# A retention recurrence with a gated feed-forward: chunk 1's rows turned by DMA, q-state products as row tiles, some stores on ScalarE, another order and other PSUM banks

## The chip, the cores and the metric

The program runs on one core of one Trainium2 chip. Its engines are TensorE (PE in the profile; its weight loads are PEld), VectorE (DVE), ScalarE (ACT), GpSimd (POOL) and SyncE (SP), which here only issues DMA. The metric is the device time of one execution in microseconds (us), the median of several runs.

## The reference

Inputs q, k, v have the shape 4 batches x 8 heads x 768 positions x 64. Each head keeps a 64x64 state that decays by a constant per position; the outputs of the recurrence are normalised over the 512 channels of a position and go through a gated feed-forward with 1536 hidden channels.

```
for t in range(S):
    state = gamma * state + einsum('bhd,bhe->bhde', k[:, :, t], v[:, :, t])
    y[:, :, t] = scale * einsum('bhd,bhde->bhe', q[:, :, t], state)
x = y.transpose(0, 2, 1, 3).reshape(B * S, H * D)
xn = x / sqrt(mean(x * x, -1) + 1e-6) * rms_g
out = (silu(xn @ w_gate) * (xn @ w_val)) @ w_out
```

## The kernel before

The 768 positions are cut into 6 chunks of 128, and a piece of work is named by chunk and batch, `c.b`. Within a chunk the recurrence is attention with a decay mask; between chunks a state is carried. The text `ORDER` (lines 17 to 93) lists every operation in the order in which the code issues it; there is no scheduler behind it. Each engine works through its own operations in that order, and waits only where it reads what another engine writes, or overwrites what another engine still reads. A word such as `g.0.3.4.0.3/3` has the operation, its arguments, and behind the stroke the PSUM banks that its result gets; `@D`, `@A`, `@P`, `@S` name the engine VectorE, ScalarE, GpSimd or SyncE, where there is a choice. PSUM has eight banks, numbered 0 to 7 here, and a product that gets a bank waits until the last reader of that bank's former content is done. The operations that matter:

- `L` loads q, k or v (from POOL as bf16, from SP as float32); `Cq` and `V` then multiply q or v by its decay (`C`, lines 330 to 337; `V`, 345 to 356).
- `Tq`, `Tk` transpose on TensorE (lines 364 and 369), `Eq`, `Ek` copy the result out of PSUM; `tq`, `tk` do the same by a DMA transpose on SP's queue (line 385).
- `A` multiplies q and k (line 401, each head pair as two groups of 64 rows), `M0`, `M1` mask the result on VectorE (423).
- `Y` (lines 428 to 443) adds the product of mask and v (438) and the product of q and the carried state (442, four full-width matmuls per batch). `Z` (line 414) makes the latter for two batches at once in 16 matmuls on 64 rows each; a `Y` of such a pair has a fourth number and only the eight matmuls of line 433.
- `S` sums squares on ScalarE (455), `R` makes the root on POOL (465, 467), `N` writes the normalised rows xn on VectorE (479). `X` transposes xn on TensorE (492) and `XE@A`, `XE@D` copy it to xnT (500); `XE@S` does both by one DMA transpose (498), without `X`.
- `K` makes the state's increment (525), `U` adds it (534), `B` casts it (541).
- `g` and `v` are the two feed-forward products (549), with chunk, hidden blocks from and to, batches from and to; `s` is Silu on ScalarE (560), `h` the gated product hT on VectorE (568). Three buffers hold `s`.
- `d` and `e` are the output product (575, 597), `o` copies it out of PSUM (140), `st` stores it (588).
- `H` are matmuls without use in the result at the start.

Chunk c+1's recurrence runs between the feed-forward products of chunk c. A q or v load of chunk 2 on SP's queue waits for the last piece of w_out (line 313).

Of the kernel before, what the change touches and what calls it, by code (L numbers as in the profile page):

```python
# [27 lines left out]
wv.9.12 h.0.0.2.0.1 s.0.4.5.0.3 v.0.0.4.3.4/2 g.0.0.4.3.4/7 v.0.4.5.0.3/3 mc.1@P s.0.5.6.0.3 s.0.0.4.3.4 h.0.0.4.3.4
wo.0.4 v.0.5.6.0.3/4 h.0.5.6.0.3 D.1.1@P Lv.1.1@P h.0.4.5.0.3 Lv.1.0@P g.0.8.9.0.4/7 g.0.6.7.0.4/0 mc.0@D s.0.8.9.0.4
v.0.4.6.3.4/4 g.0.4.6.3.4/5 s.0.4.6.3.4 v.0.8.9.0.4/6 D.1.0@D D.1.2@P wo.4.8 s.0.6.7.0.4 Tk.1.2/2 Ek.1.2@D Tq.1.0/5  # L30
g.0.7.8.0.4/1 Eq.1.0@D h.0.8.9.0.4 v.0.6.7.0.4/7 h.0.4.6.3.4 wo.8.12 v.0.7.8.0.4/3 s.0.7.8.0.4 h.0.6.7.0.4
g.0.11.12.0.4/5 s.0.11.12.0.4 Tk.1.0/7 h.0.7.8.0.4 Tq.1.1/0 Lv.1.2@P Lq.1.3@P Tq.1.2/3 Eq.1.1@D B.0.1 Eq.1.2@D
g.0.9.10.0.4/4 s.0.9.10.0.4 B.0.2 g.0.10.11.0.4/2 s.0.10.11.0.4 Ek.1.0@D A.1.0/3710 M1.1.1 A.1.2/46 v.0.10.11.0.4/2
v.0.11.12.0.4/0 M0.1.2 M0.1.1 v.0.9.10.0.4/5 M0.1.0 Lv.2.0@S d.0.0.0.4/1 M1.1.0 M1.1.2 h.0.9.10.0.4 Y.1.1/3
d.0.3.0.4/6 Lk.2.3@P h.0.11.12.0.4 Y.1.0/4 S.1.1 Lk.1.3@P R.1.1 h.0.10.11.0.4 S.1.0 N.1.1 d.0.1.0.4/0 R.1.0
d.0.2.0.4/5 N.1.0 X.1.1/3 d.0.2.4.8 d.0.0.4.8 Lv.1.3@P d.0.3.4.8 X.1.0/7 d.0.3.8.12 XE.1.0@A Y.1.2/2 Tq.1.3/7
d.0.0.8.12 S.1.2 d.0.1.4.8 Lq.2.0@S XE.1.1@D o.0.0@A Eq.1.3@D o.0.3@A R.1.2 N.1.2 Tk.1.3/1 d.0.2.8.12 X.1.2/3 Ek.1.3@A
# [5 lines left out]
V.2.0@D tq.2.0 g.1.0.4.3.4/0 B.1.0 v.1.8.9.0.4/5 h.1.9.10.0.4 Cq.2.2@P Lq.3.0@S s.1.0.4.3.4 g.1.11.12.0.4/1 tk.2.1
s.1.8.9.0.4 h.1.0.4.3.4 g.1.5.6.0.4/7 Lv.2.1@S B.1.1 h.1.8.9.0.4 v.1.5.6.0.4/0 s.1.5.6.0.4 g.1.4.5.0.4/4
g.1.10.11.0.4/5 Cq.3.1@D Lv.2.2@S v.1.11.12.0.4/7 Cq.2.3@P h.1.5.6.0.4 s.1.11.12.0.4 B.1.3 h.1.11.12.0.4
v.1.10.11.0.4/0 s.1.10.11.0.4 s.1.4.5.0.4 h.1.10.11.0.4 v.1.4.5.0.4/4 Cq.3.0@P h.1.4.5.0.4 g.1.7.8.0.4/5 Lk.3.0@P
A.2.0/4726 tq.2.3 tq.2.2 M0.2.0 v.1.7.8.0.4/0 Lv.2.3@S tq.3.1 Lk.3.2@P M0.2.1 s.1.7.8.0.4 M1.2.1 g.1.6.7.0.4/1
# [25 lines left out]
tk.5.2 Y.4.3.2 Y.4.2.2 S.4.1 h.3.7.8.0.4 v.3.11.12.0.4/7 U.4.0.2@D V.5.1@A tk.5.3 Lv.5.3@S d.3.0.0.10/3 S.4.2 XE.4.0@S
h.3.11.12.0.4 S.4.3 Cq.5.0@P d.3.0.10.12 tq.5.1 R.4.3 N.4.3 o.3.0@A tq.5.0 d.3.2.0.12/1 R.4.1 d.3.1.0.10/2 o.3.2@A
tk.5.1 R.4.2 B.4.0 N.4.1 XE.4.3@S N.4.2 XE.4.2@S V.5.0@D B.4.1 A.5.2/3514 d.3.1.10.12 d.3.3.0.12/6 XE.4.1@S M1.5.2
g.4.8.9.0.4/0 tk.5.0 B.4.3 M1.5.3 M0.5.2 v.4.8.9.0.4/4 o.3.3@D V.5.3@P s.4.8.9.0.4 B.4.2 Y.5.2/5 M0.5.3 o.3.1@A
# [560 lines left out]
```

## Time and profile before

| what | value |
|---|---|
| median of 3 runs | 232.16 us (231.9 to 232.98) |
| the profiled execution | 231.99 us |
| its span, first to last instruction | 230.3 us |
| granted TensorE clock | 1.0 |
| busy TensorE, VectorE, GpSimd, ScalarE | 224.7, 127.8, 105.7, 84.2 us |

The profile has, for each instruction, its engine, its line and its times; the timeline gives start and duration, with the idle time of the engine ahead of it in brackets. The chain is followed back from the last instruction through what released each step. Durations of single matmuls overlap, so TensorE's work is read from the pieces of the chain and from starts. What ended an engine's idle time is inferred from semaphores.

### The profile page before, as it was taken

Reading aid. Unit: us, or ns where it says so; the run is one execution under the profiler, and the core shown is the slowest. Engines: PE = TensorE matmul, PEld = TensorE weight load, DVE = VectorE, ACT = ScalarE, POOL = GpSimd, SP = SyncE. Lnnn points to the kernel's source line nnn. Section 1 sums busy time; section 2 is a strip of 40 time slices with the busy share of each in tenths; the row PEclk is TensorE's granted clock in tenths of the full one; section 3 lists DMA queues with packets and bytes.
Section 4 is the critical chain, followed back from the end, with each engine's and each line's share of the span. In section 5 each row is a group of like instructions: output and inputs, shape, how many; then the busy total and the mean of one; then the engine's idle time right before and its main releaser. Section 6 shows DMA issues by size and latency. Waiting matters only on the chain.

```text
span 230.3 us, 4745 instructions
## 1 busy us (share of the span) xinstructions
PE 224.7 (98%) x1849; PEld 118.9 (52%) x1849; DVE 127.8 (55%) x232; ACT 84.2 (37%) x190; POOL 105.7 (46%) x177
## 2 busy tenths in 40 slices
PE   8889999999999999999999999999999999999994
...
GB/s 130 162 175 134 187 176 191 199 192 134 141 180 164 156 110 180 215 187 228 184 84 288 177 179 271 132 85 90 49 23 198 101 0 0 0 16 35 45 181 92
DMA packets 105352, 31.51 MB, mean 137 GB/s; under 512 B 94449, under 2 KB 102385, under 8 KB 105330
## 3 DMA queue, kind: packets, MB, share of 16 engines
...
q8 instruction: 14, 0.23, 0.4%
q14 instruction: 8, 0.07, 0.1%
...
## 4 chain that ended last, share of the span: by engine, by line
PE 93%; DVE 2%; DMA 2%; POOL 1%; issue 0%; ACT 0%; POOLq 0%; DVEq 0%
PE v_ps L549 27%; PE g_ps L549 27%; PE o_ps L575 26%; PE a_ps L401 2%; PE y_ps L438 2%; DMA qb<-in_q_dram 2%; PE y_ps L442 2%; PE kv_ps L525 1%; PE o_ps L597 1%; DVE am L423 1%; PE t_ps L369 1%; PE xt_ps L492 1%; DVE kd L514 1%; PE t_ps L364 1%; POOL qb L307 1%; PE g_row_ps L290 0%
## 5 line engine op out<-in xcount | busy, mean ns | idle before, releaser
L568 DVE TENSOR_TENSOR hT<-sg,v_ps 128x512 bf16<-128x512 bf16 (+2 forms) x76 | 48.0, 656 | 55.4 <-PE v_ps L549 40.2
L560 ACT ACTIVATE sg<-g_ps 128x512 bf16<-128x512 f32 (+2 forms) x76 | 42.3, 575 | 93.6 <-PE g_ps L549 85.2
L549 PE MATMUL g_ps<-xnT,wg_b 128*128 128x512 bf16 (+2 forms) x344 | 71.1, 344 | 0.0
L549 PE MATMUL v_ps<-xnT,wv_b 128*128 128x512 bf16 (+2 forms) x344 | 71.0, 344 | 0.0
L575 PE MATMUL o_ps<-wo_b,hT 128*128 128x512 bf16 x276 | 63.4, 379 | 0.0
L549 PEld LDWEIGHTS <-wg_b 128*128 128x128 bf16 x344 | 30.6, 98 | 29.9 <-issue 0.3
L549 PEld LDWEIGHTS <-wv_b 128*128 128x128 bf16 x344 | 30.5, 98 | 29.1 <-DVE hT L568 0.2
L575 PEld LDWEIGHTS <-hT 128*128 128x128 bf16 x276 | 26.3, 98 | 29.7
L465 POOL TENSOR_SCALAR ms<-ssq 128x1 f32<-128x1 f32 x24 | 4.5, 188 | 42.0 <-ACT xsq L455 41.1
L423 DVE TENSOR_TENSOR am<-a_ps,causal 128x512 bf16<-128x512 f32 x32 | 20.1, 684 | 3.2 <-PE a_ps L401 3.2
L479 DVE SCALAR_TENSOR_TENSOR xn<-y_ps,rstd,g_bc 128x512 bf16<-128x512 f32 x22 | 16.4, 749 | 9.8 <-POOL rstd L467 8.0
L541 POOL CAST st_b<-st_f 64x256 bf16<-64x256 f32 x40 | 18.1, 452 | 5.4 <-DVE st_f L534 4.1
L455 ACT ACTIVATE xsq<-y_ps 128x512 f32<-128x512 f32 x22 | 13.1, 598 | 15.6 <-PE y_ps L442 14.1
L309 POOL DMA_DIRECT2D kb<-in_k_dram x20 | 18.4, 921 | 0.0
L140 ACT COPY o_sb<-o_ps 128x512 f32<-128x512 f32 (+1 forms) x15 | 8.4, 568 | 24.0 <-PE o_ps L575 23.7
L337 POOL TENSOR_TENSOR qb<-qf,ydec 128x512 bf16<-128x512 f32 x13 | 13.9, 1069 | 5.0 <-DMA qf<-in_q_dram 2.3
L467 POOL TENSOR_TENSOR rstd<-ms,mhalf 128x1 f32<-128x1 f32 x24 | 13.3, 555 | 2.0
L140 DVE COPY o_sb<-o_ps 128x512 f32<-128x512 f32 (+2 forms) x11 | 6.7, 622 | 13.3 <-PE o_ps L575 7.6
L356 POOL TENSOR_TENSOR vp<-vf,vdec 128x512 bf16<-128x512 f32 x9 | 9.3, 1046 | 3.7 <-DMA vf<-in_v_dram 3.5
L423 DVE TENSOR_TENSOR am<-a_ps,mask 128x512 bf16<-128x512 f32 x16 | 9.9, 682 | 1.6 <-PE a_ps L401 1.5
L438 PEld LDWEIGHTS <-am 128*128 128x128 bf16 x176 | 7.7, 98 | 3.5
L234 PE MATMUL hot_ps<-one 128*128 128x512 bf16 x23 | 7.9, 491 | 1.1 <-DVE one L147 1.1
...
## 6 DMA issues: line engine op xcount, KB each, us to landing
...
```

The source lines that it names most:

```text
L140: return (e.copy if e is ACT else e.tensor_copy)(out, in_)
L309: i = done[n, c, b] = e.dma_start(out=x, in_=rows[n][b, c])
L337: e.tensor_tensor(out=u["qb"], in0=u["qf"], in1=ydec[:, c, :, None].to_broadcast([128, H, D]), op=ALU.mult)
L423: return DVE.tensor_tensor(out=u["am"][:, i], in0=u["a"][i], in1=m, op=ALU.mult)
L455: return ACT.activation(xsq, flat(u["y"]), AF.Square, accum_out=u["ssq"])
L467: return POOL.tensor_tensor(out=u["rstd"], in0=ms, in1=mhalf, op=ALU.pow)
L479: return DVE.scalar_tensor_tensor(out=u["xn"], in0=flat(u["y"]), scalar=u["rstd"], in1=g_bc, op0=ALU.mult, op1=ALU.mult)
L541: POOL.tensor_copy(st_b[b][r, :, i * 64:i * 64 + 64], st_f[b // 2][r, b % 2])
L549: r = nc.tensor.matmul(p[:, (n - n0) * m:(n - n0 + 1) * m], W[w][0][:, s, n * 128:(n + 1) * 128], xnT[c][:, s, b0 * C:b1 * C], start=s == ...
L560: return ACT.activation(sg[:, :cols], done["wg", c, n0, b0][:, :cols], AF.Silu)
L568: return DVE.tensor_tensor(out=hT[c][:, n0:n1, b0 * C:b1 * C], in0=sg, in1=p, op=ALU.mult)
L575: nc.tensor.matmul(o_ps[c, b], hT[c][:, n, b * C:(b + 1) * C], wo_b[:, n, :], start=n == 0, stop=n == NFF - 1)
```

## The change

The code is the same; the text `ORDER` is another. It has the same operations but for these:

- `X.1.0` to `X.1.3` are gone, and `XE.1.0` to `XE.1.3`, two on ScalarE and two on VectorE before, are now `@S`, DMA transposes.
- `Z.2.0`, `Z.3.0`, `Z.4.0` and `Z.5.2` are new, and their eight Y take the shorter form; with `Z.4.2`, which was there, five pairs have their q-state products as row tiles.
- Fourteen `st` move from `@S` to `@A`; four `Cq` go from POOL to VectorE and some `V` and `o` change engines.
- `Tk.1.3`, the transpose of chunk 1's last k, stands in both orders, on TensorE.
- Up to `M0.1.0` the sequence is the same and only the banks differ; behind it the sequence is another.

The diff is one of the table alone. Some of its lines: its first, the one with `g.0.3.4.0.3` in the head, one of chunk 1's feed-forward, and two with a new Z:

```diff
-Lk.0.2@S H.4/4 yd causal Lv.0.2@S>causal yt rms.1@S ident Ck.0.2@A Lq.0.0@P H.8/1 Lq.0.1@P Lq.0.2@P Tk.0.2/7 H.2/5
...
-v.0.3.4.0.3/3 v.0.2.3.0.3/4 N.0.3 g.0.3.4.0.3/0 Lk.1.2@P s.0.0.2.0.1 X.0.3/6 v.0.0.2.0.1/5 XE.0.3@A Lk.1.0@P B.0.0
...
-U.1.2.2@D d.0.1.8.12 Cq.2.1@P s.1.3.4.0.3 U.1.0@D g.1.2.3.0.3/2 v.1.0.1.0.3/5 N.1.3 Lq.3.1@S s.1.1.2.0.3 X.1.3/3
...
+Lk.0.2@S H.4/0 yd causal Lv.0.2@S>causal yt rms.1@S ident Ck.0.2@A Lq.0.0@P H.8/1 Lq.0.1@P Lq.0.2@P Tk.0.2/0 H.2/1 Lk.0.0@P
...
+v.0.2.3.0.3/6 N.0.3 g.0.3.4.0.3/3 Lk.1.2@P s.0.0.2.0.1 X.0.3/5 v.0.0.2.0.1/2 XE.0.3@A Lk.1.0@P B.0.0 wg.9.12
...
+v.1.2.3.0.3/2 v.1.1.2.0.3/0 Cq.2.1@D s.1.3.4.0.3 s.1.0.1.0.3 Lk.2.1@P XE.1.3@S Lq.2.3@S Lk.2.0@P tq.2.1 h.1.3.4.0.3
+Cq.2.3@D g.1.10.11.0.4/5 s.1.1.2.0.3 s.1.2.3.0.3 g.1.8.9.0.4/6 v.1.0.4.3.4/7 tq.2.0 h.1.1.2.0.3 h.1.0.1.0.3 Lk.3.0@P
...
+h.1.5.6.0.4 A.2.2/2317 Lv.2.3@S Lv.2.2@S Lk.3.1@P Z.2.0/64 Lq.3.0@S M1.2.0 Y.2.1.2 V.2.2@D h.1.7.8.0.4 M0.2.2 tk.3.1
...
+s.2.5.6.0.4 Z.3.0/21 s.2.2.3.0.4 Y.3.0.2 v.2.4.5.0.4/0 h.2.7.8.0.4 Lv.3.3@S V.3.1@D h.2.5.6.0.4 s.2.1.2.0.4
```

In the head, TensorE's rows from the last v product ahead of `g.0.3.4.0.3` on (this one is the product of line 549 with wg; the brackets name the semaphores that a row waits for, DMASW of a load, DVE of VectorE):

```order
 L549 MATMUL v_ps<-xnT,wv_b 128x384
 L549 LDWEIGHTS wg_b [waits DMASW6_49]
+L549 MATMUL g_ps<-xnT,wg_b 128x384 [waits DVE_49]
+L549 LDWEIGHTS wg_b
 L549 MATMUL g_ps<-xnT,wg_b 128x384
```

With bank 3 in place of bank 0, the product waits for VectorE.

SP's queue behind the three transfers of the start, before (vf and qf are loads of chunks 2 and 3, kT and qT their transposes):

```order
L309 DMA vf<-in_v_dram 128x8x64
L309 DMA qf<-in_q_dram 128x8x64 x3
L385 DMA_TRANSPOSE kT<-kb 128x4x128
L309 DMA qf<-in_q_dram 128x8x64
L385 DMA_TRANSPOSE kT<-kb 128x4x128
```

And after, at the same place:

```order
L498 DMA_TRANSPOSE xnT<-xn 128x4x128
L309 DMA vf<-in_v_dram 128x8x64
L309 DMA qf<-in_q_dram 128x8x64
L498 DMA_TRANSPOSE xnT<-xn 128x4x128 x2
L309 DMA qf<-in_q_dram 128x8x64 x2
L498 DMA_TRANSPOSE xnT<-xn 128x4x128
L309 DMA qf<-in_q_dram 128x8x64
L385 DMA_TRANSPOSE qT<-qb 128x4x128 x3
```

The four transposes of chunk 1's rows are new there, and the loads of q stand between and behind them; the last of the four q loads is `Lq.2.3`.

VectorE at the start of chunk 1's feed-forward, before, from the two masks of batch 3 (`M1.1.3`, `M0.1.3`) on:

```order
L423 TENSOR_TENSOR am<-a_ps,mask_102 128x512 x2
L534 TENSOR_TENSOR st_f_121<-st_f_121,kv_ps 128x256
L534 TENSOR_TENSOR st_f_122<-st_f_122,kv_ps 128x512
L534 TENSOR_TENSOR st_f_121<-st_f_121,kv_ps 128x256
L479 SCALAR_TENSOR_TENSOR xn<-y_ps,rstd,g_bc 128x512
L568 TENSOR_TENSOR hT<-sg,v_ps 128x384
L140 COPY xnT<-xt_ps 128x4x128
L568 TENSOR_TENSOR hT<-sg,v_ps 128x384 x3
```

And after:

```order
L423 TENSOR_TENSOR am<-a_ps,mask_102 128x512 x2
L140 COPY o_sb<-o_ps 128x512
L534 TENSOR_TENSOR st_f_122<-st_f_122,kv_ps 128x512
L140 COPY o_sb<-o_ps 128x512
L534 TENSOR_TENSOR st_f_121<-st_f_121,kv_ps 128x256
L479 SCALAR_TENSOR_TENSOR xn<-y_ps,rstd,g_bc 128x512
L337 TENSOR_TENSOR qb<-qf,ydec 128x512
L568 TENSOR_TENSOR hT<-sg,v_ps 128x384
L337 TENSOR_TENSOR qb<-qf,ydec 128x512
L568 TENSOR_TENSOR hT<-sg,v_ps 128x384 x3
```

Two `o`, and the q products `Cq.2.1` and `Cq.2.3`, now stand on VectorE among the first h of chunk 1; the copy of xnT is gone.

More of the change, by code (lines that the diff above doesn't have):

```diff
@@ L28 @@
[L28 to L37, printed above, removed]
@@ L43 @@
[L43 to L47, printed above, removed]
@@ L73 @@
[L73 to L76, printed above, removed]
-A.5.0/2067 Y.5.3/3 S.5.3 h.4.8.9.0.4 g.4.0.1.0.4/4 M0.5.1 M1.5.1 v.4.7.8.0.4/1 M1.5.0 M0.5.0 g.4.7.8.0.4/7 S.5.2
@@ new lines @@
+v.0.5.6.0.3/4 h.0.5.6.0.3 D.1.1@P Lv.1.1@P h.0.4.5.0.3 Lv.1.0@P g.0.8.9.0.4/6 g.0.6.7.0.4/4 mc.0@D s.0.8.9.0.4
+v.0.4.6.3.4/3 g.0.4.6.3.4/6 s.0.4.6.3.4 v.0.8.9.0.4/0 D.1.0@D D.1.2@P wo.4.8 s.0.6.7.0.4 Tk.1.2/6 Ek.1.2@D Tq.1.0/2
+g.0.7.8.0.4/4 Eq.1.0@D h.0.8.9.0.4 v.0.6.7.0.4/6 h.0.4.6.3.4 wo.8.12 v.0.7.8.0.4/0 s.0.7.8.0.4 h.0.6.7.0.4
+g.0.11.12.0.4/4 s.0.11.12.0.4 Tk.1.0/6 h.0.7.8.0.4 Tq.1.1/0 Lv.1.2@P Lq.1.3@P Tq.1.2/3 Eq.1.1@D B.0.1 Eq.1.2@D
+g.0.9.10.0.4/2 s.0.9.10.0.4 B.0.2 g.0.10.11.0.4/0 s.0.10.11.0.4 Ek.1.0@D A.1.0/2634 M1.1.1 A.1.2/51 v.0.10.11.0.4/7
@@ new lines @@
+v.3.9.10.0.4/2 h.3.1.2.0.4 s.3.6.7.0.4 v.3.4.5.0.4/5 g.3.3.4.0.4/0 h.3.0.1.0.4 Lq.4.3@S Lk.4.2@P h.3.6.7.0.4 B.3.3
+s.3.9.10.0.4 tk.4.1 tq.4.0 v.3.3.4.0.4/6 o.2.3@A g.3.4.5.0.4/4 B.3.1 Cq.4.3@P st.2.2@A tq.4.1 st.1.0@A s.3.3.4.0.4
+s.3.4.5.0.4 Lv.4.0@S h.3.3.4.0.4 h.3.9.10.0.4 B.3.2 Lq.4.2@S g.3.2.3.0.4/0 h.3.4.5.0.4 tk.4.0 A.4.0/4261 Lv.4.2@S
+Z.4.0/37 g.3.10.11.0.4/5 M1.4.1 s.3.2.3.0.4 V.4.0@P Lv.4.1@S M1.4.0 v.3.2.3.0.4/1 M0.4.1 Lq.5.3@S g.3.8.9.0.4/2
+Cq.4.2@P M0.4.0 s.3.8.9.0.4 v.3.10.11.0.4/4 s.3.10.11.0.4 tk.4.2 tq.4.3 tq.4.2 V.4.2@P Y.4.0.2 Lv.4.3@S h.3.2.3.0.4
@@ new lines @@
+v.3.8.9.0.4/2 S.4.0 tk.4.3 g.3.7.8.0.4/5 s.3.7.8.0.4 g.3.11.12.0.4/1 R.4.0 h.3.8.9.0.4 Lq.5.2@S Cq.5.3@P h.3.10.11.0.4
+s.3.11.12.0.4 V.4.3@A Lv.5.3@S V.5.3@P N.4.0 A.4.2/5426 V.4.1@D d.2.0.0.10/0 Y.4.1.2 M0.4.2 K.4.0.2/5 K.4.2.2/1 M1.4.2
+Cq.5.2@P S.4.1 M1.4.3 M0.4.3 Z.4.2/26 Y.4.3.2 U.4.2.2@D U.4.0.2@D B.4.0 v.3.7.8.0.4/4 Y.4.2.2 h.3.7.8.0.4 tk.5.2
+d.2.0.10.12 v.3.11.12.0.4/5 st.1.3@A S.4.3 R.4.3 tk.5.3 h.3.11.12.0.4 d.3.0.0.10/4 tq.5.2 N.4.3 R.4.1 N.4.1
+d.3.3.0.12/5 XE.4.0@S o.2.0@A S.4.2 tq.5.3 XE.4.3@S A.5.2/7301 R.4.2 XE.4.1@S N.4.2 XE.4.2@S d.3.1.0.10/6 tk.5.1
```

106 lines of the change are left out of this document (54 added, 52 removed).

## The prediction

> **What bounds the kernel now.** I read the page's busy shares first, then the chain that ended last, then, place by place, the timeline of TensorE beside that of the engine that hands over to it.
>
> ```profile
> PE 224.7 (98%) x1849; PEld 118.9 (52%) x1849; DVE 127.8 (55%) x232; ACT 84.2 (37%) x190; POOL 105.7 (46%) x177
> ...
> PE   8889999999999999999999999999999999999994
> ...
> PE 93%; DVE 2%; DMA 2%; POOL 1%; issue 0%; ACT 0%; POOLq 0%; DVEq 0%
> ```
>
> TensorE is busy in every slice behind the head, and 93% of the chain is TensorE itself. What a busy TensorE delivers is seen in the pieces of the chain (start, duration, line, number of matmuls):
>
> ```profile
> 60.42 0.22 PE xt_ps L492 x4
> ...
> 74.95 0.61 PE a_ps L401 x16
> 75.56 0.97 PE v_ps L549 x4
> 76.53 0.86 PE g_ps L549 x4
> ...
> 82.33 0.23 PE y_ps L438 x8
> 82.57 0.22 PE y_ps L442 x4
> ...
> 148.11 0.63 PE kv_ps L525 x32
> 148.74 0.34 PE y_ps L414 x16
> 149.08 0.97 PE v_ps L549 x4
> ...
> 182.15 2.59 PE g_ps L549 x12
> ```
>
> Twelve 512-column matmuls in 2.59 us are 0.216 us each, and a group of four takes 0.86 everywhere from 17 us to the end: before has no stall there to win back. The time is the sum of TensorE's work plus what a new order makes it wait. So there are two questions: how much work goes, and where TensorE now waits.
>
> **Work that goes.** The four X of chunk 1 (16 transposes) go: 4 x 0.22 = 0.88 us. Eight Y lose their four L442 matmuls (8 x 0.22 = 1.76), and four new Z add 0.34 each (1.36): 0.40 less, of which Z.3.0, standing alone between full-width products, gives back 0.11 (the product behind a 64-row group takes 0.97, not 0.86; Z.2.0, Z.4.0 and Z.5.2 lie against an A that pays this already): 0.28. K.1.1, now alone between two d pieces, costs a change in and out, an estimate of twice 0.11; K.2.2.2 joins the other K of chunk 2 and saves 0.1: +0.15 with the small rest. Together -1.0 us, with an error of 0.2.
>
> The row prices two tiles of q-state products at 0.34 against 0.44 for the full-width pair. The Trainium skill (TensorEngine Tiling (Array Packing), Theoretical Speedup) allows up to 2x for a contraction of 64; by it a Z would take 0.22 and the sum would come out 0.5 lower. The same page (Key Properties) says that a change of tiling mode drains the array, which speaks against scattered Z; the 0.11 behind L414 agrees with it. The sum goes by the rows.
>
> **Waits in the head.** Up to `M0.1.0` the operations are the same, but their PSUM banks are not: the head of after uses seven banks (bank 7 first at `v.0.10.11.0.4/7`), so a product often gets a bank whose reader has not finished. For each reuse I took the end of the reader and the start of the product from the timelines of before:
>
> ```profile
> 19.28 0.41 DVE L568 TENSOR_TENSOR hT<-sg,v_ps 128x256 bf16<-128x256 bf16 x1
> 19.93 0.42 DVE L140 COPY xnT<-xt_ps 128x512 bf16<-128x512 bf16 x1 [0.24 <-PE xt_ps L492]
> 21.92 0.75 DVE L479 SCALAR_TENSOR_TENSOR xn<-y_ps,rstd,g_bc 128x512 bf16<-128x512 f32 x1 [0.74 <-POOL rstd L467]
> 28.21 1.69 DVE L568 TENSOR_TENSOR hT<-sg,v_ps 128x512 bf16<-128x512 bf16 x3 [1.66 <-ACT sg L560]
> 33.39 0.41 DVE L140 COPY kT<-t_ps 128x512 bf16<-128x512 bf16 x1
> 34.32 0.67 DVE L568 TENSOR_TENSOR hT<-sg,v_ps 128x512 bf16<-128x512 bf16 x1
> ...
> 19.51 0.39 PE L492 MATMUL xt_ps<-ident,xn 128*128 128x128 bf16 x4
> 20.41 0.28 PE L549 MATMUL g_ps<-xnT,wg_b 128*128 128x128 bf16 x2
> 22.17 0.81 PE L549 MATMUL g_ps<-xnT,wg_b 128*128 128x384 bf16 x4
> 33.47 1.89 PE L549 MATMUL v_ps<-xnT,wv_b 128*128 128x512 bf16 x8
> 36.22 0.73 PE t_ps L369 x12
> ```
>
> A product starts 0.05 us behind the end it waits for (copy done 20.35, product 20.41). Then:
> - `X.0.0/5` gets the bank of `v.0.0.2.2.3/5`, read until 19.69: it starts at 19.74, not 19.50: +0.24.
> - `g.0.3.4.0.3/3` gets the bank of Y.0.3, whose reader N.0.3 ends at 22.67 (POOL sets that, so it doesn't move): 22.72, not 22.17 + 0.24: +0.31. TensorE is now 0.55 late.
> - VectorE's queue from 28.2 on starts with a wait on ScalarE's reading of a g product, so it moves by the same 0.55. `v.0.6.7.0.4/6` waits for the kT copy, 33.80 + 0.55 + 0.05 = 34.40, not 33.47 + 0.55: +0.38.
> - `v.0.7.8.0.4/0` (the second four of the eight at 33.47) waits for the hT product that ends at 34.99 + 0.55 + 0.05 = 35.59, not 34.33 + 0.93: +0.33.
> - The transposes at 36.22 hold 0.07 of an old wait (three times 0.22 is 0.66), which vanishes.
>
> Sum +1.2 us; nothing ahead of the product stream swallows it. Its bounds: 0 if the readers were all earlier for a reason I don't see, 1.6 if VectorE's queue slips more.
>
> **Waits at chunk 1's rows.** In before the rows reach xnT by TensorE and a copy; now by `XE.1.*@S`. From Y.1.3 to the end of its N, before:
>
> ```profile
> 56.33 0.40 PE L438 MATMUL y_ps<-vp,am 128*128 128x64 bf16 x8
> ...
> 57.07 0.60 ACT L455 ACTIVATE xsq<-y_ps 128x512 f32<-128x512 f32 x1 [0.70 <-PE y_ps L442]
> ...
> 58.19 0.56 POOL L467 TENSOR_TENSOR rstd<-ms,mhalf 128x1 f32<-128x1 f32 x1
> ...
> 58.79 0.75 DVE L479 SCALAR_TENSOR_TENSOR xn<-y_ps,rstd,g_bc 128x512 bf16<-128x512 f32 x1 [1.74 <-ACT sg L560]
> 61.40 1.49 DVE L568 TENSOR_TENSOR hT<-sg,v_ps 128x384 bf16<-128x384 bf16 x3
> ```
>
> That is 59.54 - 56.33 = 3.21 us. DMA times, first of all xnT transposes, then of those at 111 to 120, then of all q loads, then of the two q loads at 58 to 64, and the q product on VectorE (ns):
>
> ```profile
> L498 SPq DMA_TRANSPOSE xnT<-xn x16: 1189/1207/1801, 83.2 to 175.5; - x16
> DMA to landing us min/median/max: 2.4/2.5/5.2
> ...
> DMA to landing us min/median/max: 3.8/4.7/5.2
> ...
> L337 DVE TENSOR_TENSOR qb<-qf,ydec x3: 678/684/781, 68.2 to 140.9; 128x512 bf16<-128x512 f32 x3
> DMA to landing us min/median/max: 3.3/4.5/6.5
> ...
> DMA to landing us min/median/max: 3.3/3.3/3.4
> ```
>
> - Batch 2: from Y.1.2 to `g.1.2.3.0.3` the new order has 6.5 us of TensorE work (five d pieces of 0.86, two Y of 0.45, two transposes of 0.22, A at half of 0.61, K at three quarters of 0.63). Needed: 3.2 + 2.4 to 5.2. Slack 0.9 to -1.9; at the median 0.8.
> - Batch 3: from Y.1.3 to `g.1.10.11.0.4` 0.45 + 0.86 + 8 x 0.65 = 6.5. The same slack.
> - VectorE: `Cq.2.3@D` now stands ahead of three h, and its load `Lq.2.3@S` behind `XE.1.3@S` in SP's queue. From Y.1.3: 3.21 + 1.2 (the issue of XE) + load + 0.68 + two h of 0.5, then TensorE's `g.1.0.4.3.4/4` takes the bank that the second h frees; with hops of 0.1 that is 6.2 + load against 6.5 + 0.86 + 0.86 + 0.89 + 0.86 = 10.0. A load of 3.8 is free; 3.3 leaves 0.5, the median 4.5 costs 0.7, the longest 6.5 costs 2.7.
>
> I take +0.3 for the three together, because the rows nearest in time (3.3) are harmless; bounds 0 and +2.7.
>
> **Other handovers.** Behind chunk 3's last Y, TensorE has 36 x 0.216 + 0.45 = 8.2 us before `g.3.1.2.0.4`; needed are 3.2 + 1.2 (XE.3.3 ahead of XE.3.2 in the queue) + 2.4 to 5.2: slack 1.4 to -1.4. Chunks 2 and 5 are alike. I take +0.2, bounds 0 and +2.
>
> **Edits at nothing.** Fourteen stores are issued by ScalarE:
>
> ```profile
> L588 SPq DMA_DIRECT2D out_dram<-o_sb x26: 332/447/1516, 89.6 to 227.5; - x26
> ```
>
> Their issue on ScalarE isn't in the trace; on SP it takes 0.33 to 1.52 us. ScalarE is 37% busy, and its idle time between Silus hides it; a Silu queued behind a store delays h and a bank. Bounds: 0, and 14 x 0.45 = 6 us if every one lay on the path; I take 0, the row of the last copies being near: st.5.3.2 is issued before o.5.3.0 can start. The last transfer is again 192 columns, so the tail keeps its shape. Tk.1.3 stays on TensorE in both orders, so "its last k" costs and gives nothing. V and Cq change places between POOL and VectorE, neither of them the bound.
>
> **Sum.** The profiled execution took 231.99 us (span 230.3). 231.99 - 1.0 + 1.2 + 0.3 + 0.2 = 232.7; the median of before lies 0.17 above that execution, so 232.8.
>
> **Rivals.**
> - Slower by VectorE's wait for `Lq.2.3`: one mechanism, at `Cq.2.3@D`. It decides when the load takes over 4.8 us (then 1 us more than my sum, 233.8); at 6.5 it gives 235.3. For it: the median load of 4.5. Against: 3.3 at just this time. 0.14.
> - Slower by handovers of chunks 2, 3 and 5 with landings as at 111 to 120: some 2 us, 234.6. For it: 3.8 to 5.2 there. Against: 2.4 where DMA is idle. 0.18.
> - Faster, since the bank waits of the head are covered by something: 231.99 - 1.0 + 0.2 = 231.2, a little lower with a better tail. Against: the wait stands in the program, and the reader's end is set by other engines. 0.12.
> - Z at half price: 232.3, which changes no sign; L414's own row is against it. 0.02.
>
> **How the numbers follow.** My forecast has 0.54. A half per cent, 1.16 us, is about what a measurement of this kernel can tell from no change: faster is below 231.0, slower above 233.3. Faster: most of the third rival, 0.10. Slower: the first two, 0.32. The rest, 0.58, within. The range runs from 231.2 (no head waits) to 234.8 (the handovers, or a load of 6). The forecast's own is 231.9 to 233.3.
>
> **What would show it.** Right: TensorE idle for about 0.3 us each behind xn at 22.7, behind the kT copy near 34.3 and hT near 35.5; L492 with 16 fewer matmuls; Z groups at 0.34; a 512-column matmul still at 0.216. Wrong: no TensorE wait before 40 us (then faster); VectorE idle on a q load near 62 to 65 us with TensorE idle behind it, or long waits at the first products of chunks 3 and 5 (then slower); ScalarE's queue held by stores.

## The result, and the profile after

| kernel | median | executions | ratio to before, 95% interval |
|---|---|---|---|
| before | 232.09 us | 231.9 to 232.98 | |
| changed | 235.79 us | 234.69 to 236.39 | 1.0143, 1.011 to 1.0176 |

The change makes the kernel 1.4% slower; the time lies above the range of the prediction. Medians here and below are of all executions of a kernel, ratios leave out those more than 1.5% above its fastest. The profiled execution of the changed kernel took 234.69 us (span 233.0), the shortest of its four. Its page, by busy shares, slices and the chain that ended last:

```profile
PE 223.4 (96%) x1865; PEld 116.5 (50%) x1865; DVE 129.5 (56%) x242; ACT 83.8 (36%) x198; POOL 102.5 (44%) x180
...
PE   7799999999999999899998999999999999999994
...
PE 78%; DMA 9%; DVE 5%; POOL 3%; ACT 2%; issue 1%; SPq 1%; POOLq 0%; ACTq 0%
```

TensorE's busy time is less (223.4 against 224.7 us), but its share of the chain fell from 93% to 78%, and DMA's rose from 2% to 9%. TensorE now waits, and two of its 40 slices in the middle are no longer full. The timeline of TensorE shows where (in brackets the idle time ahead of a row and what is taken to have ended it; a wait inside a row only makes the row longer):

```profile
22.39 0.81 PE L549 MATMUL g_ps<-xnT,wg_b 128*128 128x384 bf16 x4
...
33.54 2.20 PE L549 MATMUL v_ps<-xnT,wv_b 128*128 128x512 bf16 x8
...
56.98 1.30 PE L549 MATMUL g_ps<-xnT,wg_b 128*128 128x384 bf16 x7 [0.51 <-DMA xnT<-xn]
...
94.17 1.02 PE L549 MATMUL v_ps<-xnT,wv_b 128*128 128x512 bf16 x4 [1.54 <-ACT o_sb L140]
...
127.09 1.67 PE L549 MATMUL g_ps<-xnT,wg_b 128*128 128x512 bf16 x7 [1.05 <-DMA xnT<-xn]
```

The last three are the first feed-forward products of chunks 1, 2 and 3: `g.1.2.3.0.3`, `v.2.3.4.0.4` and `g.3.1.2.0.4`. Counted from start to start, less the usual length of the group ahead, they wait 0.67, 1.72 and 1.21 us. In the head, row by row against before, the only new wait over 0.14 us is inside the eight matmuls at 33.54 (2.20 where 1.89 is usual): 0.31. Sum 3.9 us. `e.5.3.0`, the last output product, starts 2.53 us later than before (228.48 against 225.95), so 1.4 us of work went: chunk 1's X 1.0, Y 1.7 less 1.2 for the new Z, and 0.2 at A less 0.3 at v.

The chain of the changed kernel has the rows of chunks 1 and 3, with the transposes in it:

```profile
51.98 0.75 DVE xn L479
...
52.76 4.09 DMA xnT<-xn
...
56.98 0.32 PE g_ps L549
...
123.06 3.89 DMA xnT<-xn
...
127.09 1.02 PE g_ps L549 x4
```

And VectorE's timeline has the ends of N, from which each transpose can start (750 ns for a full row, L479), and in the head the readers of the banks:

```profile
21.59 0.75 DVE L479 SCALAR_TENSOR_TENSOR xn<-y_ps,rstd,g_bc 128x512 bf16<-128x512 f32 x1 [0.36 <-POOL rstd L467]
...
33.05 0.41 DVE L140 COPY kT<-t_ps 128x512 bf16<-128x512 bf16 x1
...
33.98 1.60 DVE L568 TENSOR_TENSOR hT<-sg,v_ps 128x512 bf16<-128x512 bf16 x3
...
88.32 0.75 DVE L479 SCALAR_TENSOR_TENSOR xn<-y_ps,rstd,g_bc 128x512 bf16<-128x512 f32 x1 [0.95 <-POOL rstd L467]
...
117.95 0.75 DVE L479 SCALAR_TENSOR_TENSOR xn<-y_ps,rstd,g_bc 128x512 bf16<-128x512 f32 x1
...
120.66 0.75 DVE L479 SCALAR_TENSOR_TENSOR xn<-y_ps,rstd,g_bc 128x512 bf16<-128x512 f32 x1 [0.76 <-POOL rstd L467]
```

In chunk 3, N.3.2 is done at 118.70, but its transpose stands behind that of N.3.3 in SP's queue (done 121.41) and is issued at 123.06. In chunk 2, N.2.3 is done at 89.07; its transpose is issued at 89.80, as the third of three that take 1.2 us each on SP. The three chunk-2 transposes (L498 in the view of DMA: issue in ns, first and last start; then issue to landing in us) before and after:

```profile
L498 SPq DMA_TRANSPOSE xnT<-xn x3: 1196/1198/1216, 85.8 to 88.4; - x3
...
DMA to landing us min/median/max: 2.4/2.4/2.5
```

```profile
L498 SPq DMA_TRANSPOSE xnT<-xn x3: 1216/1216/1217, 87.2 to 89.8; - x3
...
DMA to landing us min/median/max: 3.1/3.7/4.3
...
L309 POOL DMA_DIRECT2D kb<-in_k_dram x3: 873/955/963, 86.4 to 91.8; - x3
```

The same transposes land in 2.4 us before and in up to 4.3 us after, where loads of k are issued at 86.4, 90.0 and 91.8 us (last row).

### The profile page after: what moved, and what is told of

Same layout as the page of the kernel before. It is cut to its first block, busy times and chain, and to the rows that moved or that the text cites. A ratio compares the mean times of both kernels' runs of the same rounds, so it can differ in the third digit from the quotient of the medians.

```text
span 233.0 us, 4788 instructions
## 1 busy us (share of the span) xinstructions
PE 223.4 (96%) x1865; PEld 116.5 (50%) x1865; DVE 129.5 (56%) x242; ACT 83.8 (36%) x198; POOL 102.5 (44%) x180
## 4 chain that ended last, share of the span: by engine, by line
PE 78%; DMA 9%; DVE 5%; POOL 3%; ACT 2%; issue 1%; SPq 1%; POOLq 0%; ACTq 0%
PE g_ps L549 25%; PE v_ps L549 24%; PE o_ps L575 17%; DMA xnT<-xn 5%; PE a_ps L401 2%; DMA qf<-in_q_dram 2%; DMA qb<-in_q_dram 2%; POOL rstd L467 1%; DVE hT L568 1%; PE y_ps L438 1%; PE y_ps L433 1%; PE o_ps L597 1%; PE t_ps L364 1%; DVE xn L479 1%; PE kv_ps L525 1%
## 5 line engine op out<-in xcount | busy, mean ns | idle before, releaser
L560 ACT ACTIVATE sg<-g_ps 128x512 bf16<-128x512 f32 (+2 forms) x76 | 42.4, 576 | 84.5 <-PE g_ps L549 58.8
L549 PE MATMUL v_ps<-xnT,wv_b 128*128 128x512 bf16 (+2 forms) x344 | 70.0, 344 | 1.7 <-ACT o_sb L140 1.5
L549 PE MATMUL g_ps<-xnT,wg_b 128*128 128x512 bf16 (+2 forms) x344 | 69.6, 344 | 1.6 <-DMA xnT<-xn 1.6
L541 POOL CAST st_b<-st_f 64x256 bf16<-64x256 f32 x40 | 17.4, 436 | 19.4 <-DVE st_f L534 15.4
L140 ACT COPY o_sb<-o_ps 128x512 f32<-128x512 f32 (+2 forms) x17 | 9.2, 552 | 22.2 <-PE o_ps L575 20.3
L455 ACT ACTIVATE xsq<-y_ps 128x512 f32<-128x512 f32 x14 | 8.4, 597 | 20.0 <-PE y_ps L442 16.0
L140 DVE COPY o_sb<-o_ps 128x512 f32<-128x512 f32 (+1 forms) x9 | 5.9, 651 | 13.9 <-PE o_ps L575 8.0
L337 POOL TENSOR_TENSOR qb<-qf,ydec 128x512 bf16<-128x512 f32 x9 | 9.3, 1038 | 9.5 <-PE g_ps L549 6.7
L479 DVE SCALAR_TENSOR_TENSOR xn<-y_ps,rstd,g_bc 128x512 bf16<-128x512 f32 x14 | 10.5, 748 | 3.0 <-POOL rstd L467 2.6
L452 ACT ACTIVATE xsq<-y_ps 128x256 f32<-128x256 f32 x20 | 7.5, 381 | 12.3 <-PE y_ps L433 11.0
L464 POOL TENSOR_TENSOR ssq<-ssq 128x1 f32<-128x1 f32 x10 | 1.9, 190 | 20.3 <-ACT xsq L452 20.3
```

The source lines that it names most:

```text
L140: return (e.copy if e is ACT else e.tensor_copy)(out, in_)
L337: e.tensor_tensor(out=u["qb"], in0=u["qf"], in1=ydec[:, c, :, None].to_broadcast([128, H, D]), op=ALU.mult)
L479: return DVE.scalar_tensor_tensor(out=u["xn"], in0=flat(u["y"]), scalar=u["rstd"], in1=g_bc, op0=ALU.mult, op1=ALU.mult)
L541: POOL.tensor_copy(st_b[b][r, :, i * 64:i * 64 + 64], st_f[b // 2][r, b % 2])
L549: r = nc.tensor.matmul(p[:, (n - n0) * m:(n - n0 + 1) * m], W[w][0][:, s, n * 128:(n + 1) * 128], xnT[c][:, s, b0 * C:b1 * C], start=s == ...
L560: return ACT.activation(sg[:, :cols], done["wg", c, n0, b0][:, :cols], AF.Silu)
```

## The experiments

**Theory.** The loss is the handover of rows to xnT by DMA, and a handover has three parts: the chain from Y to the end of N, the place in SP's queue, and the landing (the time from the transpose's issue to the arrival of its data), which loads in flight stretch. **Rivals**: the PSUM banks of the head, the stores on ScalarE, or something else at the same places (the profile names ScalarE's copy o.1.1 at chunk 2).

### Chunk 3: the order of two transposes

```diff
-XE.3.1@S Lq.4.1@S d.2.3.0.12/4 XE.3.3@S XE.3.2@S
+XE.3.1@S Lq.4.1@S d.2.3.0.12/4 XE.3.2@S XE.3.3@S
```

> The changed kernel with XE.3.2 ahead of XE.3.3 in SP's queue; nothing else moves. In its profile TensorE waits 1.21 us ahead of g.3.1.2.0.4 (127.09) for the transpose that SP issues at 123.06, although N.3.2 ends at 118.70; the transpose ahead of it in the queue waits for N.3.3, to 121.41. Theory (order of the queue): XE.3.2 goes at 118.8, XE.3.3 at 121.4 and lands 3.5 us later at 124.9, ahead of the 125.9 at which TensorE comes: the wait goes, -1.2 us. Rival (the landing under load sets it, whatever the order): a landing of 5.2 us gives 126.6, and -0.5 us or less.

Measured: 234.42 us, ratio 1.0093 (1.0071 to 1.0115), 0.5% less than the changed kernel. TensorE's timeline and the two transposes:

```profile
126.74 2.54 PE L549 MATMUL g_ps<-xnT,wg_b 128*128 128x512 bf16 x11 [0.28 <-DMA xnT<-xn]
```

```profile
L498 SPq DMA_TRANSPOSE xnT<-xn x2: 1202/1206/1211, 119.9 to 121.9; - x2
...
DMA to landing us min/median/max: 4.8/5.5/6.3
```

The wait falls from 1.21 to 0.44 us. Theory and rival each named a part: the order gave 0.8, and landings of 4.8 and 6.3 us, among two stores on ScalarE, two loads of k and one of q, kept 0.4. The profiled execution (234.36 us) is only 0.33 us shorter than that of the changed kernel, since TensorE is 0.4 us later here already at the d pieces ahead (118.53 against 118.11).

### Chunk 2: one row by TensorE

```diff
-d.1.1.10.12 A.3.0/2563 o.1.1@A
+d.1.1.10.12 X.2.3/3 XE.2.3@A A.3.0/2563 o.1.1@A
...
-M0.3.1 B.2.3 XE.2.3@S B.2.0
+M0.3.1 B.2.3 B.2.0
```

> The changed kernel with one row of chunk 2, batch 3, turned on TensorE (X.2.3, four matmuls ahead of A.3.0) and copied by ScalarE in place of XE.2.3 on SP. In the changed kernel TensorE waits 1.72 us ahead of v.2.3.4.0.4 (94.17); the last transpose is issued at 89.80 and lands at 94.08. Theory (the handover of this one row is late): the wait goes but for what XE.2.0 (issued 88.49, landed 91.62) leaves, +0.22 for the four matmuls, so -1.5 us. Rival (the wait is for something else that stands there, the bank or ScalarE's copy o.1.1, which the profile names as releaser): the wait stays, and the time is +0.2 us.

Measured: 233.46 us, ratio 1.0051 (1.0027 to 1.0074). The first product of chunk 2 has no wait any more:

```profile
93.32 1.03 PE L549 MATMUL v_ps<-xnT,wv_b 128*128 128x512 bf16 x4
```

0.5 us stand instead inside A.3.0, whose last bank waits for the copy of the new X. The wait was for this one row, not for o.1.1: ScalarE's copy, the name behind the arrow, had ended at 93.26 in the changed kernel, 0.9 us before the product started.

### Chunk 2: the loads taken away

```diff
-R.2.0 Lk.5.0@P R.2.3
+R.2.0 R.2.3
...
-v.2.8.9.0.4/5 Lk.3.3@P B.2.1
+v.2.8.9.0.4/5 B.2.1
...
-s.2.8.9.0.4 Lk.4.0@P g.2.1.2.0.4/7
+s.2.8.9.0.4 g.2.1.2.0.4/7
...
-V.3.0@P Cq.3.2@P
+V.3.0@P Lk.4.0@P Lk.5.0@P Lk.3.3@P Cq.3.2@P
```

> The changed kernel with three loads of k (Lk.5.0, Lk.3.3, Lk.4.0; 86.4, 90.0 and 91.8 us on POOL) moved behind V.3.0 in POOL's queue, so that they start behind 97 us. The last transpose of chunk 2 is then alone with the loads of SP. Theory A (the landing of 4.28 us at 89.80 is stretched by loads in flight; the same transposes in the kernel before landed in 2.4): it lands in about 2.5 to 3 us, and TensorE's wait of 1.72 us falls to 0.2 to 0.7, so -1.0 to -1.5 us. Theory B (the queue and the chain set it): R.2.3 is 0.7 us earlier on POOL, but XE.2.3 still goes at 89.8 behind its two neighbours in SP's queue, the landing stays, and the time moves by less than 0.3 us.

Measured: 234.54 us, ratio 1.0091 (1.006 to 1.0121). The three transposes, in the same view as above, and the first product:

```profile
L498 SPq DMA_TRANSPOSE xnT<-xn x3: 1216/1216/1217, 87.8 to 90.5; - x3
...
DMA to landing us min/median/max: 2.4/2.4/2.4
```

```profile
93.07 1.03 PE L549 MATMUL v_ps<-xnT,wv_b 128*128 128x512 bf16 x4
```

The last transpose goes even later than in the changed kernel (90.5 against 89.8 us), yet lands in 2.4 us, and the whole wait of 1.72 us is gone: theory A. A wait of 0.46 us stands ahead of `g.1.10.11.0.4` at 62.8 us; this is well before the loads that were moved, so it is not shown to come from them.

### Before: the loads put in

The other direction, in the kernel before:

```diff
-R.2.3 N.2.3
+R.2.3 Lk.3.3@P Lk.4.1@P N.2.3
...
-d.1.1.0.10/5 Lk.3.3@P V.2.3@P
+d.1.1.0.10/5 V.2.3@P
...
-g.2.3.4.0.4/2 Lk.4.1@P o.1.3@D
+g.2.3.4.0.4/2 o.1.3@D
```

> The kernel before with two loads of k (Lk.3.3 and Lk.4.1) moved to directly behind R.2.3 on POOL, so that they start at about 87.6 and 88.5 us, beside chunk 2's transposes, which land there in 2.42 to 2.50 us. Nothing else changes. Theory (a load in flight stretches a transpose's landing): the last of chunk 2's transposes lands in 4 us or more, as in the changed kernel, and TensorE, which comes 1.5 us behind that landing in the kernel before, waits 0 to 0.5 us. Rival (the landing is longer in the changed kernel for another reason): it stays at 2.4 to 2.6 us.

Measured, one profiled execution of 232.1 us. The transposes and the loads:

```profile
L498 SPq DMA_TRANSPOSE xnT<-xn x3: 1189/1196/1217, 85.4 to 88.1; - x3
...
DMA to landing us min/median/max: 2.4/2.4/4.3
...
L309 POOL DMA_DIRECT2D kb<-in_k_dram x2: 892/928/963, 87.2 to 88.2; - x2
```

The third transpose, issued at 88.06 between loads at 87.19 and 88.16, lands in 4.29 us. The second, issued at 86.71, half a microsecond ahead of the first load, keeps 2.44. TensorE waits 0.48 us. So it is the loads, in both kernels, and the kernel before had a slack of 1.5 us that paid for them.

### Chunk 1: one row back on TensorE

```diff
-XE.1.0@S XE.1.2@S Cq.2.0@P
+XE.1.0@S Cq.2.0@P
...
-Y.1.3/4 d.0.2.8.12
+Y.1.3/4 X.1.2/0 XE.1.2@A d.0.2.8.12
```

> The changed kernel with one row of chunk 1, batch 2, turned on TensorE again (X.1.2 behind Y.1.3, copied by ScalarE) in place of XE.1.2 on SP, the other three rows of chunk 1 by DMA as in the change. In the changed kernel TensorE waits 0.67 us ahead of g.1.2.3.0.3 for that transpose (issued 52.76, landed 56.85). Theory (the handover alone): the wait of 0.67 goes, 0.22 comes, -0.45 us. Rival (freed time is eaten at the next row, XE.1.3, or its loads): 0 to +0.2 us, with a new wait ahead of g.1.10.11.0.4.

Measured: 235.59 us, ratio 1.0135 (1.0105 to 1.0164), no gain that can be told. The product of batch 2 starts at 56.50 without a wait, and the next one takes it over:

```profile
62.97 1.25 PE L549 MATMUL g_ps<-xnT,wg_b 128*128 128x512 bf16 x4 [1.11 <-DMA xnT<-xn]
```

That is the new wait that the rival named, 1.27 us long: XE.1.3 is issued at 58.74 and lands 4.2 us later. About half of the wait is the 0.67 us by which TensorE now comes earlier. The other half is the edit's own: ScalarE makes the new copy (0.58 us, L140) ahead of batch 3's squares, and N.1.3 ends at 58.71 rather than 58.13. So batch 3's handover had little slack in the changed kernel; its landing there is not in the trace.

### The head's banks

```diff
-v.0.2.3.0.3/6 N.0.3 g.0.3.4.0.3/3
+v.0.2.3.0.3/4 N.0.3 g.0.3.4.0.3/0
```

> The changed kernel with the PSUM banks of the kernel before in the head (up to v.0.9.10.0.4), the banks behind it renamed so that each reuse stays the same; no operation moves. The prediction's term: TensorE waits 1.2 us in the head for these banks, so -1.2 us. What the trace of the changed kernel shows: A.1.0 starts at 38.92 against 38.61 before, 0.31 us ahead of v.0.7.8.0.4 the only wait, so -0.3 us or less, and no change of the three waits behind (0.67, 1.72 and 1.21).

Measured: 235.54 us, ratio 1.0143 (1.01 to 1.0187), the same as the changed kernel. A.1.0 starts at 38.53 against 38.93. So the banks cost some 0.4 us, not 1.2: the seven traced kernels with the changed kernel's banks start A.1.0 at 38.4 to 39.2, the seven with the banks of before at 37.9 to 38.9. Its trace also shows something new. The wait of chunk 3 was longer here (2.26 us), and behind it (for each stretch its length, TensorE's busy time and matmuls, the granted clock, the DMA engines' share and GB/s):

```profile
127.58 4.44 PE L549 MATMUL g_ps<-xnT,wg_b 128*128 128x512 bf16 x12 [2.10 <-DMA xnT<-xn]
```

```profile
126.00:127.00 1.00, 0.00 (x0) 1.00 1.81 223
127.00:128.00 1.00, 0.42 (x2) 0.98 1.34 241
128.00:129.00 1.00, 1.00 (x4) 0.50 0.98 215
129.00:130.00 1.00, 1.00 (x4) 0.50 0.26 57
130.00:131.00 1.00, 1.00 (x3) 0.50 0.89 205
131.00:132.00 1.00, 1.00 (x5) 0.81 1.27 286
```

TensorE's clock is 0.50 for some 3.4 us, which costs 1.7 us more than the wait itself.

### The stores back on SP

```diff
-st.1.2@A N.3.2 st.1.1@A s.2.9.10.0.4
+st.1.2@S N.3.2 st.1.1@S s.2.9.10.0.4
```

All fourteen are changed so.

> The changed kernel with all its stores on SP's queue at the same places of the order; none on ScalarE. Theory (the prediction's: the issue of a store on ScalarE is hidden): within 0.3 us of the changed kernel, and the three waits of TensorE stay. Rival 1 (stores on ScalarE hold Silu, their bytes crowd the transposes of chunk 3): -0.5 us or more. Rival 2 (on SP they stand ahead of transposes and loads): +0.5 us or more, with a longer wait ahead of g.3.1.2.0.4, since st.1.1 and st.1.2 then stand ahead of XE.3.1.

Measured: 235.89 us, ratio 1.0163 (1.0126 to 1.0199): not to be told from the changed kernel. The waits stay (0.60, 1.59 and 1.07 us). Chunk 3's two transposes have no store beside them now, and still land in 3.4 and 4.2 us (3.5 and 3.9 in the changed kernel): it is not the stores that stretch them there. Only the end differs: `e.5.3.0` starts 0.7 us earlier, and the span is 1.2 us longer, since the last stores now all stand on SP, seven in one row:

```profile
224.80 6.27 SPq L588 DMA_DIRECT2D out_dram<-o_sb  x7
```

### One part alone: chunk 1's rows by DMA in the kernel before

```diff
-N.1.2 Tk.1.3/1 d.0.2.8.12 X.1.2/3 Ek.1.3@A
+N.1.2 XE.1.2@S Tk.1.3/1 d.0.2.8.12 Ek.1.3@A
...
-A.1.3/17 XE.1.2@A M1.1.3
+A.1.3/17 M1.1.3
```

The other three rows alike.

> The kernel before with one part of the change alone: chunk 1's four rows go by XE.1.*@S, each right behind its N, and X.1.* are gone; no other operation moves. -0.88 us for 16 transposes. Theory (a handover by DMA needs some 3.2 + 4 us behind the last Y, and the order of before leaves less): N.1.2 ends at 53.4 and would land at about 57, where TensorE without the X comes at 54.5: 2.5 us of wait, and as much again ahead of the first product of batch 3: +2 to +4 us. Rival (the transposes land in 2.4 us and TensorE's other work covers them): -0.9 to +0.5 us.

Measured: 239.51 us, ratio 1.0303 (1.0266 to 1.0341), 7 us slower, the only kernel here whose whole interval lies above 2%:

```profile
58.55 0.80 PE L549 MATMUL g_ps<-xnT,wg_b 128*128 128x384 bf16 x2 [4.36 <-DMA xnT<-xn]
...
68.96 1.02 PE L549 MATMUL g_ps<-xnT,wg_b 128*128 128x512 bf16 x4 [1.98 <-DMA xnT<-xn]
```

4.5 and 2.1 us of wait, and 1.75 us of half clock behind the first. The mechanism is the theory's, the sum was too low by the longer first wait and the clock. The new order of chunk 1 takes most of this away: the transposes without it are worse.

### All handovers mended, first attempt

```diff
-d.0.1.4.8 d.0.0.4.8 h.0.11.12.0.4 B.1.1 Y.1.2/4
+d.0.1.4.8 h.0.11.12.0.4 Y.1.2/4 d.0.0.4.8 B.1.1
...
-d.0.3.8.12 Y.1.3/4 d.0.2.8.12
+d.0.1.8.12 Y.1.3/4 d.0.3.8.12 d.0.2.8.12
...
-XE.1.1@S Tk.1.3/0 d.0.1.8.12 Lv.2.0@S Ek.1.3@A A.1.3/04 Lq.2.0@S K.1.0/2 XE.1.0@S XE.1.2@S
+XE.1.1@S Tk.1.3/0 d.0.0.8.12 Ek.1.3@A A.1.3/04 K.1.0/2 XE.1.0@S XE.1.2@S Lv.2.0@S Lq.2.0@S
```

> The changed kernel with all three handovers mended. Chunk 1: Y.1.2 stands one d piece earlier, Y.1.3 too (d.0.3.8.12 behind it), D.1.3 on POOL, the loads Lv.2.0 and Lq.2.0 behind XE.1.2, and Cq.2.0 and Lk.2.3 behind R.1.3. Chunk 2: the three loads of k behind V.3.0. Chunk 3: XE.3.2 ahead of XE.3.3, and the loads Lk.4.1 and Lk.5.1 behind the window. Theory (these waits are the whole loss): TensorE's waits of 0.67, 1.72 and 1.21 us go, -3.6 us against the changed kernel, so about 0.3 us slower to 1.0 us faster than the kernel before. Rival (a wait mended comes back at the next handover): at most half of it, so 1 to 2 us slower than the kernel before, with new waits ahead of g.1.10.11.0.4 or at the loads of chunk 3 and 4.

Measured: 237.5 us (234.54 to 239.26), ratio 1.0141 (1.0095 to 1.0188): the rival; nothing of the gain is left. The trace is of an execution of 238.49 us, and the shorter ones have none, so it may show more waits than they have. In it the three waits are 0.25, 0 and 0, but chunk 1's first batch-3 product, the q and k of chunk 3, and the k of chunk 4 are late. First TensorE's timeline, then the chain at 57 to 64 us:

```profile
63.61 1.67 PE L549 MATMUL g_ps<-xnT,wg_b 128*128 128x512 bf16 x6 [1.13 <-DVE hT L568]
...
112.71 0.62 PE L401 MATMUL a_ps<-qT,kT 64*128 64x128 bf16 x16 [1.32 <-DMA qT<-qb]
...
149.64 0.40 PE L401 MATMUL a_ps<-qT,kT 64*128 64x128 bf16 x8 [1.79 <-DMA kT<-kb]
```

```profile
57.58 4.72 DMA qf<-in_q_dram
...
62.40 0.06 DVE qb L337
...
63.01 0.56 DVE hT L568
```

Loads that I had moved out of one handover, or that stand behind those in a queue, were late for their own use: Lq.2.1 holds `Cq.2.1@D`, which stands ahead of an h on VectorE; the k loads land in 6 to 8 us at 98 to 110, and their transposes are late.

### All handovers mended, with less moved

```diff
-N.1.0 Eq.1.3@D N.1.2 d.0.2.4.8
+N.1.0 N.1.2 Eq.1.3@D d.0.2.4.8
...
+s.1.3.4.0.3 R.1.3 U.1.0@D N.1.3 X.1.3/1 XE.1.3@D
...
-XE.3.3@S XE.3.2@S
+XE.3.2@S XE.3.3@S
...
-s.2.9.10.0.4 Lk.5.1@P S.3.3 Lk.4.1@P
+s.2.9.10.0.4 S.3.3 Lk.4.1@P
...
-V.5.3@P N.4.0
+V.5.3@P Lk.5.1@P Lk.5.0@P N.4.0
```

> The changed kernel with its handovers mended without crowding others. Chunk 1: Y.1.2 one d piece earlier and N.1.2 ahead of Eq.1.3 on VectorE, batch 3's row by X.1.3 on TensorE with its copy on VectorE, Cq.2.1 behind the first h. Chunk 2: Lk.5.0 and Lk.4.0 moved away and Lk.3.3 one cast later on POOL. Chunk 3: XE.3.2 ahead of XE.3.3, Lk.5.1 moved to about 149 us. The head's banks are those of before. Theory (the loss is these waits, each set by a transpose issued late or landing among loads): waits of 0.67, 1.72 and 1.21 us fall to 0 to 0.3 each, 0.22 comes for X.1.3: about 231.5 to 232.5 us, 0.2 us either side of the kernel before, and 1 to 1.5 us below the row e2_row23. Rival (freed time is eaten by the next handover, as in e7_mended): 233.5 to 235.5 us with new waits ahead of A.3.2 or g.1.10.11.

Measured: 231.93 us, ratio 0.9989 (0.996 to 1.0018): the theory's time, 1.5% below the changed kernel. Some 0.4 us of this may be the head's banks, which are those of before here. TensorE's timeline has no wait at the first products of chunks 2 and 3:

```profile
91.49 1.03 PE L549 MATMUL v_ps<-xnT,wv_b 128*128 128x512 bf16 x4
...
123.63 2.54 PE L549 MATMUL g_ps<-xnT,wg_b 128*128 128x512 bf16 x11
```

0.41 us remain at chunk 1, and 0.58 ahead of the second half of A.5.0 at 167.9. A further 0.43 are inside the d pieces at 117, where stores hold ScalarE, and a Silu (L560) starts behind their issue:

```profile
113.74 2.62 ACTq L588 DMA_DIRECT2D out_dram<-o_sb  x2
...
116.41 0.60 ACT L560 ACTIVATE sg<-g_ps 128x512 bf16<-128x512 f32 x1 [2.09 <-DVE xn L479]
```

### Two more steps

The kernel above, with `X.1.2` on TensorE, the two stores behind the Silu, and one store later on SP:

```diff
-st.1.2@A N.3.2 st.1.1@A s.2.9.10.0.4
+N.3.2 s.2.9.10.0.4 st.1.2@A st.1.1@A
...
-Lq.5.1@S st.2.1@S d.3.2.0.12/1
+Lq.5.1@S d.3.2.0.12/1
...
-tq.5.0 v.4.9.10.0.4/0 tq.5.1
+tq.5.0 v.4.9.10.0.4/0 tq.5.1 st.2.1@S
```

> The kernel e9_handover with its three remaining waits of TensorE addressed: batch 2's row of chunk 1 by X.1.2 on TensorE with its copy on ScalarE (in place of the wait of 0.41 us ahead of g.1.2.3; 0.22 comes), the stores st.1.2 and st.1.1 behind the Silu s.2.9.10 on ScalarE (in its trace two stores hold ScalarE's queue for 2.6 us, and TensorE waits 0.43 us for the h behind that Silu), and st.2.1 behind tq.5.1 on SP (0.61 us ahead of A.5.0's second half). Theory (each wait has the cause named): 0.2 + 0.4 + 0.6 = 1.2 us less, about 230.8 us, 0.5% faster than the kernel before. Rival (the next handover eats it): 231.5 to 232 us, no faster than before.

Measured: 236.6 us, ratio 1.0204 (1.0176 to 1.0233). Up to 165 us TensorE has no wait behind the head; then VectorE's copy `o.3.2` waits for the buffer of the very store that was moved, and `Z.5.2` for the copy's bank, 3.2 us long; behind that the granted clock is 0.50 from 170.0 to 173.4. The rows of SP, VectorE and TensorE:

```profile
166.74 0.53 SPq L588 DMA_DIRECT2D out_dram<-o_sb  x1
...
169.17 0.69 DVE L140 COPY o_sb<-o_ps 128x512 f32<-128x512 f32 x1 [3.18 <-issue]
...
169.92 0.58 PE L414 MATMUL y_ps<-st_b,qT 64*128 64x64 bf16 x16 [3.08 <-DVE o_sb L140]
```

The kernel with that one store put back:

```diff
-tq.5.0 v.4.9.10.0.4/0 tq.5.1 st.2.1@S
+tq.5.0 v.4.9.10.0.4/0 tq.5.1
```

> The kernel e11_handover2 with one store put back: st.2.1 stands ahead of tk.5.0 on SP, as in the changed kernel. In e11_handover2 TensorE waits 3.24 us ahead of Z.5.2 for VectorE's copy o.3.2, which starts at 169.17, when the late store (issued 166.74) has released one of six buffers; behind that wait matmuls run at half clock for 1.8 us. Up to g.4.5.6 at 165.8 that kernel has no wait. Theory (the late store alone made the wait): 3.2 + 1.8 us go, 231.0 to 231.6 us, 0.3 to 0.5% faster than the kernel before, with 0.4 to 0.6 us of wait left ahead of A.5.0's second half. Rival (another wait takes its place ahead of Z.5.2): 232 us or more.

Measured: 232.0 us, ratio 1.0009 (0.9984 to 1.0034). The wait ahead of Z.5.2 is gone, so the late store made it. TensorE's waits are 1.2 us, all in the head and at A.5.0. The expected 231.0 to 231.6 was missed by 0.4: in the profiled execution 0.4 us came in at `g.0.3.4.0.3`, where the load of wg was late. The time is the rival's, but no wait took the place that it named. No version is measurably faster than the kernel before; two are equal to it.

## Why the prediction was wrong

- **Other handovers, +0.2 us: the step that failed.** It measured 1.7 (chunk 2) and 1.2 (chunk 3), 2.9 in all. The slack of chunk 3 had been worked out as 1.4 to -1.4 us, with the right parts, and then the end with a landing of 2.4 us was taken; the landings that TensorE waited for took 4.28 and 3.89. "Chunks 2 and 5 are alike" was not worked out. Chunk 2's sum, from Y.2.3 at 85.31: 3.76 to the end of N.2.3 (a load of k stands ahead of R.2.3 on POOL), 0.73 for the queue, 4.28 for the landing and 0.09 to the start, 8.86, against 7.14 us of TensorE work: 1.72. Chunk 3's, from Y.3.3 at 117.64: 3.77 to the end of N.3.3, 1.65 for the queue, 3.89 for the landing and 0.14 to the start, 9.45, against 8.24: 1.21. The prediction had 3.2 and 1.2 for the first two parts, so these were short as well, by 1.0 together. Each number but the landing could have been had from the order and the rows of before; the landing's upper end, 5.2, was in the quoted rows. In chunk 3 the order alone was worth 0.8, and the landings kept the rest; which of the loads of k and q beside them stretch these, no run separates. Chunks 4 and 5 have no wait at their first products.
- **Chunk 1, +0.3 us.** It measured 0.67. The batch 2 row was late, by a landing of 4.09 us; the prediction gave it 0.8 of slack at the median landing of 2.5. The load of `Cq.2.3` took 4.1 us and VectorE idled 1.99 us for it, but no wait of TensorE followed, so the first rival did not come here. In the kernels with moved loads the same mechanism came at `Cq.2.1`, up to 1.3 us.
- **Head, +1.2 us.** It measured 0.3 by the trace, and the experiment on the banks shows no difference in time. The mechanism is right where it acts: g.0.3.4 starts at 22.39, 0.05 behind N.0.3 (21.59 + 0.75), and v.0.7.8 starts at 34.71, 0.05 behind the first hT of 33.98. The sizes were off: N.0.3 came 0.33 us earlier than before, which the prediction had excluded ("POOL sets that, so it doesn't move"), and so the product waited little and VectorE's queue didn't slip. Ahead of the kT copy two rows (L276, L514) also took 3.2 us together where before has 3.7, so this copy (33.05 + 0.41) was done ahead of v.0.6.7 at 33.54. That part is luck of the execution: in the seven traces with these banks the copy starts at 32.6 to 33.3, and the wait of 0.3 at `v.0.7.8.0.4` is in three of them. One late step had been handed on twice in the sum.
- **Work, -1.0 us.** It measured -1.4. X was 1.0; a Z is 0.33 (0.24 where it stands ahead of A) and the Y pairs gave 0.5 rather than 0.28; K cost nothing, where +0.15 had been put.
- **Stores, 0.** The experiment cannot tell them from 0 in the sum. But a Silu behind two stores was late once (the second mended kernel), the case that the prediction had named. With two queues the end takes 4.5 us from the start of `e.5.3.0`, with SP alone 6.4 in this order.
- The sum by the trace: -1.4 + 0.3 + 0.7 + 2.9 = +2.5, and 0.2 at the end, which is 2.7 us between the two profiled executions (234.69 - 231.99). The other executions of the changed kernel are 0.6 to 1.7 us longer; they have no trace, so that part stays open. One that is 1.7 us longer has a mean granted clock of 0.992, as a stretch of half clock behind a wait would give; another, 1.6 us longer, has 1.0, so this is not all of it.
- The second rival (handovers of chunks 2 and 3, 234.6 us) was the right one, and at 234.69 for the profiled execution nearly to the number. That the number fits is luck: the rival had 2 us where chunks 2 and 3 alone cost 2.9, and a head of 1.2 that measured 0.3 makes up for it; the median is 1.2 us higher. It got 0.18, since the median of a transpose's landings (2.5 us) was taken as its usual price. The landings of 2.4 to 2.5 us were those of moments with no load of k in flight, and the new order has such loads there.
